# The two-block model on one core: products with v taken as one scheduled step for a pair of heads and a group, changes of form counted in the plan, and whole norms for the scales of w_in

## The chip, the core and the metric

The kernel runs on one core of a Trainium2 chip. The metric is device time in microseconds of one launch, from one execution of the program; several executions are timed and the median is used. The engines are TensorE (PE in the profile, with its weight loads as PEld), VectorE (DVE), ScalarE (ACT), GpSimd (POOL) and SyncE (SP), which here does nothing but issue transfers for the DMA engines.

## The reference, cut to what matters

Attention that is causal in blocks of 64 tokens, a dense layer with an elu between its two products, and a layer of eight experts of which each chosen token visits one:

```python
# q, k, v: (4, 8, 576, 64); x below: (2304, 512)
scores = np.matmul(q, k.transpose(0, 1, 3, 2)) / np.sqrt(D)
scores = np.where(block_i >= block_j, scores, -1e9)
attn = softmax(scores)
x = np.matmul(attn, v)                       # -> (2304, 512)
h = x @ w_in                                 # w_in (512, 2048), float64 in memory
g = np.where(h > 0.0, h, np.exp(np.minimum(h, 0.0)) - 1.0)
x = g @ w_out                                # w_out (2048, 512), float64 in memory
do_compute = x @ w_skip > 0
e_idx = np.argmax(x @ w_gate, axis=1)        # for the tokens with do_compute
out = x + gate_w * (relu(x @ w1[e_idx]) @ w2[e_idx])
```

## The kernel before

**How the work is cut.** The eight heads of a batch element `b` are four pairs `p`. Its nine blocks of 64 tokens are groups `g`: blocks 0 to 3, 4 to 7 and 8 for `b` = 0, and 0 to 3 and 4 to 8 for the others. For every block of a pair TensorE makes scores `s`, VectorE their maximum `mx`, ScalarE the exponential `e`; then the exponentials, scaled, are split into a high and a low fp16 half `ehl`. Two neighbouring blocks share one `ehl`, and a DMA transposes it into `et` (for the first group of `b` = 0 TensorE does that, through `tp`). `y` in the code is such a couple of blocks: 0 and 1 in the first group, 2 to 4 in the second. `pv` multiplies `et` with the split `vt` into the PSUM tile `xps`, which has one buffer (tag `pv`), and ScalarE and VectorE move that into `xt`, the transposed input of the dense layer. The products with v use 64 columns of the array at a time, two heads side by side; so do the scores of block 8. All the rest uses 128 columns. The table `ET_BUFS = 1, 1, 2, 1, 2` gives the number of buffers of `et` for `y` = 0 to 4.

**The dense layer** goes over nine chunks `c` of 256 tokens. `l1` makes `h`, `l1a` and `l1b` the elu `g`, `l2` makes `y`. For the first two chunks the products are in fp32, with `twi` and `two`; from the third on they are three fp16 products of split halves, with `win` and `wout`. The weights come as float64: `raw_load(x)` fetches one of 32 pieces of 512 KB into a raw buffer `rw` (16 pieces of w_in, then 16 of w_out), and `conv(x)` makes fp32 of it with three VectorE instructions. `load_to(n)` issues the loads up to number `n`. The split needs a power of two as a scale for each eighth of w_in. `sq_win(j)` squares the eighth on ScalarE into `sq` (tag `k1`, one buffer, which the splitting of k uses too), adds the squares over the rows of the matrix with four matmuls by ones into `cn` (tag `pv` again), and takes the largest column sum on VectorE. `scale_win` makes the scales of the eight maxima, once. `sq_wout` and `scale_wout` do it in another way for w_out: ScalarE adds up the squares of each partition while it makes them (`accum_out`), and one matmul by ones adds the partitions.

**What sets the order.** Nothing is issued directly. Each instruction is recorded by a `Recorder` as a step, with a time estimate and the tiles that it reads and writes; consecutive TensorE calls are one step until `rc.atom()` ends it. `order()` plays the steps through in a simulated time: at each turn it takes the engine that is free first and of its ready steps the one with the lowest due number, where `rc.base = -300` makes a step due earlier. The steps are then issued in the order of their simulated starts, so each engine's queue is fixed, and the real engines work it off in order, waiting where the plan was wrong. Due numbers come from the program order, which is a list of slots: attention units run ahead of the dense layer by a quota (`SHARE`, `CHUNKS`). TensorE's instructions and all others that pass through the recorder carry the line of its call, L310, in the profile. In `pv` each `y` has an `rc.atom()` ahead of it, so it is a step of its own. `vmax(b)` squares the whole of v of one batch element on ScalarE (`vflat`) for v's scale.

**The end.** After the dense layer the tokens are routed, and the experts follow (`ahead_block`, `block`), from about 606 us on.

Of the kernel before, what the change touches and what calls it, by code (L numbers as in the profile page):

```python
# [34 lines left out]
class Recorder:  # L35
# [15 lines left out]
    def begin(self):  # L51
        self.steps = []
        self.hist = {}
        self.users = {}
        self.rings = {}
        self.masks = {}
        self.cur = None
        self.last_pe = None
        self.shift = self.base = 0
        self.direct = False  # L60
        self.urgent = False
        self.urg = []
        self.late = {}
        self.ready = {}

    def pool(self, p):
        return _Pool(self, p)
# [84 lines left out]
    def order(self):  # L152
# [15 lines left out]
                succ[j].append(i)  # L168
        est = [self.ready.get(i, 0.0) for i in range(n)]
        free = dict(self.late)  # L170
        cand = {}
        dma_free = 0.0
        lanes = []
# [14 lines left out]
        while len(done) < n:  # L188
# [43 lines left out]
            if e == "sp":  # L232
                if len(lanes) >= 8:
                    t = max(t, lanes[-8])
                end = max(t + (1.12 if s[1] < 0.6 else 1.3), dma_free) + s[2]
                dma_free = end
                lanes.append(end + 0.9)
                free[e] = t + s[1]
            else:
                end = t + s[1]  # L240
                if e is not None:
                    free[e] = end
                end += s[2]
# [47 lines left out]
class _Engine:  # L291
# [3 lines left out]
    def __getattr__(self, op):  # L295
        def record(*args, **kw):
            rec, e = self.rec, self.e
            if rec.direct:
                return getattr(self.real, op)(*args, **kw)
            names = {"memset": ("out",), "iota": ("out",), "tensor_copy": ("out", "in_")}.get(op, ())  # L300
            ops = dict(zip(names, args))
            ops.update(kw)
            reads, writes = [], []
            for k, x in ops.items():
                if hasattr(x, "ap") and not hasattr(x, "tensor"):
                    x = x.ap
                if hasattr(x, "tensor"):
                    (writes if k in ("out", "accum_out") else reads).append(x)
            time, dma = self.cost(op, ops)
            rec.call(e, time, lambda: getattr(self.real, op)(*args, **kw), reads, writes, dma)  # L310
        return record

    def cost(self, op, k):
# [34 lines left out]
def tile_kernel(ctx, tc, q, k, v, w_in, w_out, w_skip, w_gate, w1, w2, out):  # L348
# [99 lines left out]
    st = {}  # L448
# [61 lines left out]
    def sq_win(j):  # L510

        if j == 0:
            for nm in ("cwF", "cwS", "cwI", "cwC", "cwM", "cwG"):
                st[nm] = newcol(8).start
        sq = ap.tile([128, 4, 256], BF16, tag="k1", bufs=1, name="sq")
        rc.scalar.activation(out=sq.rearrange("p a b -> p (a b)"), in_=tw("wi", j), func=AF.Square)
        cn = misc([128, 256], "cn", "pv")
        for kk in range(4):
            rc.tensor.matmul(out=cn, lhsT=ones16, rhs=sq[:, kk], start=kk == 0, stop=kk == 3)
        rc.vector.tensor_reduce(out=col[:, st["cwF"] + j:st["cwF"] + j + 1], in_=cn, axis=AX.X, op=ALU.max)  # L520

    def scale_win():

        F_, S_, I_, C_, M_, G_ = (col[:, st[nm]:st[nm] + 8] for nm in ("cwF", "cwS", "cwI", "cwC", "cwM", "cwG"))
        scale_bits(F_, S_, I_)
        rc.vector.tensor_scalar(out=C_, in0=I_, scalar1=st["v", 1][1], scalar2=2.0 ** -14, op0=ALU.mult, op1=ALU.mult)
        rc.vector.tensor_scalar(out=M_, in0=C_, scalar1=2.0 ** 35, scalar2=1.0, op0=ALU.mult, op1=ALU.max)
# [314 lines left out]
    def pv(b, p, g):  # L842
# [3 lines left out]
        for y in range(blk[0] // 2, (blk[-1] + 2) // 2):  # L846
            et = ET.pop((b, p, y))
            n, nk = et.shape[1], et.shape[2] // 2
            c0 = (2 * y - blk[0]) * 64
            rc.atom()  # L850
            for kt in range(nk):
                for eh, vh in ((0, 0), (1, 0), (0, 1)):
                    for h in range(2):
# [462 lines left out]
    rc.base = -300  # L1316
    load_raw("k", 0, 0)
    load_raw("q", 0, 0)
    load_raw("k", 0, 1)
    load_raw("q", 0, 1)  # L1320
    vflat(0)
# [628 lines left out]
```

## Time and profile before

| | us |
|---|---|
| median of 3 runs | 755.23 |
| those runs | 749.65, 756.22, 755.23 |
| profiled execution | 757.81 |
| its span, from the first to the last instruction | 756.1 |
| around the span | 1.7 |
| mean granted clock of TensorE | 0.982 of 2.4 GHz |

The page gives for the whole span each engine's busy time, a strip of 40 slices, and the groups of instructions. Views by stretch, by wait and by time give the rest. Since every instruction has the line of the recorder, groups are told apart by the tiles that they read and write.

### The profile page before, as it was taken

Reading aid. Unit: us, or ns where it says so; the run is one execution under the profiler, and the core shown is the slowest. Engines: PE = TensorE matmul, PEld = TensorE weight load, DVE = VectorE, ACT = ScalarE, POOL = GpSimd, SP = SyncE. Lnnn points to the kernel's source line nnn. Section 1 sums busy time; section 2 is a strip of 40 time slices with the busy share of each in tenths; the row PEclk is TensorE's granted clock in tenths of the full one; section 3 lists DMA queues with packets and bytes.
Section 4 is the critical chain, followed back from the end, with each engine's and each line's share of the span. In section 5 each row is a group of like instructions: output and inputs, shape, how many; then the busy total and the mean of one; then the engine's idle time right before and its main releaser. Section 6 shows DMA issues by size and latency. Waiting matters only on the chain. (4 is left out here: it accounts for less than half of the span.)

```text
span 756.1 us, 17807 instructions
## 1 busy us (share of the span) xinstructions
PE 688.2 (91%) x6696; PEld 471.3 (62%) x6696; DVE 582.8 (77%) x1688; ACT 519.7 (69%) x1100; POOL 84.1 (11%) x122
## 2 busy tenths in 40 slices
PE   4769987899999999988999999999999999997894
PEld 3548633586467666646656666757576677675683
DVE  5987997788899998978859965899778655554662
ACT  5876555799998886877748844767366558584681
POOL 2000000001000100000100010010105033243311
PEclk9999998899999999999999999999999999999998
DMA  9899999887597999879937537927065775989951
GB/s 256 239 236 316 269 251 202 188 150 134 111 192 146 162 190 197 163 131 194 161 53 165 101 63 177 386 67 225 33 196 147 212 169 122 231 195 238 292 145 16
DMA packets 280859, 134.52 MB, mean 178 GB/s; under 512 B 250347, under 2 KB 259061, under 8 KB 280240
## 3 DMA queue, kind: packets, MB, share of 16 engines
q1 hardware_dynamic: 276560, 125.68, 73.4%
q0 software_dynamic: 4192, 7.49, 4.7%
q8 instruction: 57, 0.93, 0.5%
q14 instruction: 50, 0.41, 0.2%
HBM read 74.38 MB, written 12.75 MB: 115 GB/s over the span
## 5 line engine op out<-in xcount | busy, mean ns | idle before, releaser
L310 PE MATMUL h<-xt,win 128*128 128x256 f16 x1344 | 158.4, 273 | 1.5 <-DVE n L310 1.0
L310 PE MATMUL y<-wout,g 128*128 128x512 f16 x672 | 157.0, 381 | 0.0
L310 PEld LDWEIGHTS <-win 128*128 128x128 f16 x1344 | 128.7, 98 | 22.7 <-DVE n L310 1.1
L310 PEld LDWEIGHTS <-g 128*128 128x128 f16 x672 | 64.3, 98 | 67.8 <-issue 2.0
L310 ACT ACTIVATE e<-s,mx 128x512 f32<-128x512 f32 (+4 forms) x160 | 81.9, 514 | 29.7 <-DVE ehl L310 13.5
L310 ACT ACTIVATE ehl<-e,su 128x512 f16<-128x512 f32 (+4 forms) x160 | 80.0, 548 | 15.1 <-DVE su L310 9.5
L310 DVE SCALAR_TENSOR_TENSOR ehl<-e,su,ehl 128x512 f16<-128x512 f32 (+4 forms) x160 | 81.4, 536 | 7.8 <-ACT ehl L310 7.5
L310 DVE TENSOR_REDUCE mx<-s 128x1 f32<-128x512 f32 (+4 forms) x160 | 74.8, 474 | 15.6 <-PE s L310 15.3
L310 PE MATMUL s<-kt,qt 128*128 128x384 f16 (+5 forms) x384 | 71.3, 311 | 11.9 <-ACT e L310 10.1
L310 PE MATMUL h<-xt,twi 128*128 128x256 f32 x256 | 64.0, 406 | 1.4 <-ACT xt L310 1.4
L310 PE MATMUL y<-two,g 128*128 128x512 f32 x128 | 62.6, 626 | 0.5 <-DVE two L310 0.5
L310 PEld LDWEIGHTS <-vt 128*64 128x64 f16 x1440 | 41.4, 115 | 32.4 <-issue 26.6
L310 PE MATMUL xps<-et,vt 128*64 128x128 f16 (+1 forms) x1440 | 50.7, 220 | 11.0 <-DMA et<-ehl 6.4
L310 PEld LDWEIGHTS h<-xt,twi 128*128 128x128 f32 x256 | 50.8, 204 | 9.6 <-ACT xt L310 2.1
L310 PEld LDWEIGHTS <-p 128*128 128x128 f16 x984 | 47.0, 99 | 14.0 <-issue 6.9
L310 ACT ACTIVATE el<-h,col 128x512 f32<-128x512 f32 x56 | 38.2, 682 | 24.7 <-PE h L310 24.3
L310 ACT ACTIVATE g<-el,col 128x512 f16<-128x512 f32 x56 | 40.1, 716 | 13.5 <-DVE el L310 12.8
L310 PEld LDWEIGHTS <-qt 128*128 128x128 f16 (+1 forms) x384 | 28.8, 106 | 28.5 <-issue 13.3
L1509 DVE SCALAR_TENSOR_TENSOR p<-p,n,p 128x1024 f16<-128x1024 f32 x32 | 40.7, 1278 | 4.7 <-ACT p L1508 4.5
L310 DVE SCALAR_TENSOR_TENSOR g<-el,col,g 128x512 f16<-128x512 f32 x56 | 41.6, 742 | 2.4 <-ACT g L310 2.3
L310 DVE SCALAR_TENSOR_TENSOR el<-h,col,el 128x512 f32<-128x512 f32 x56 | 41.6, 744 | 1.6 <-DVE el L310 0.5
L310 POOL DMA_INDIRECT lst_d<-li,si x16 | 18.0, 1126 | 201.5 <-DVE li L310 100.4
(233 smaller groups left out, 1166.3 us busy)
## 6 DMA issues: line engine op xcount, KB each, us to landing
p<-in_moe_w_dram SPq DMA_DIRECT2D x49, 512.0 KB
rw<-in_moe_w_in_dram SPq DMA_DIRECT2D x16, 512.0 KB
rw<-in_moe_w_out_dram SPq DMA_DIRECT2D x16, 512.0 KB
pb<-in_moe_w_dram SPq DMA_DIRECT2D x10, 512.0 KB
vflat<-in_v_dram SPq DMA_DIRECT2D x4, 1152.0 KB
out_dram<-pay SPq DMA_DIRECT2D x18, 256.0 KB
pay_d<-pay SPq DMA_DIRECT2D x18, 256.0 KB
raw<-in_k_dram SPq DMA_DIRECT2D x16, 256.0 KB
```

What stands on the lines that cost most here:

```text
L310: rec.call(e, time, lambda: getattr(self.real, op)(*args, **kw), reads, writes, dma)
L1509: rc.call("dve", 1.2, lambda: nc.vector.scalar_tensor_tensor(out=half(1), in0=raw.t, scalar=sc, in1=half(0), op0=ALU.mult, op1=ALU.subtrac ...
```

## The change

Four things change.

- In `pv` only the first `y` of a group ends the step before it. The products of a pair of heads and a group (18 matmuls in a first group, 42 or 72 in a second) are one step, which is ready when the last of its `et` is there.
- The recorder notes for every matmul whether it is whole (over 64 columns of weights or over 64 output partitions) or half. In the plan a TensorE step costs 0.095 us more when its first matmul has another form than the last one of the step before.
- `sq_win` adds the squares of a partition on ScalarE; `scale_win` adds the partitions of all eight sums with one matmul by ones, between two small VectorE copies. The scale of an eighth comes from the norm of the whole eighth, not of its largest column. The 32 matmuls into `cn` and the eight maxima are gone.
- The first two raw loads of w_in are issued right behind the first k and q.

```diff
+        self.form = {}
@@ order
+        whole = True
...
                 end = t + s[1]
+                if i in self.form:
+                    end += 0.095 * (self.form[i][0] != whole)
+                    whole = self.form[i][-1]
@@ record
-            rec.call(e, time, lambda: getattr(self.real, op)(*args, **kw), reads, writes, dma)
+            i = rec.call(e, time, lambda: getattr(self.real, op)(*args, **kw), reads, writes, dma)
+            if op == "matmul":
+                rec.form.setdefault(i, []).append(_count(ops["lhsT"].ap[1:]) > 64 or ops["out"].ap[0][1] > 64)
@@ sq_win
-        sq = ap.tile([128, 4, 256], BF16, tag="k1", bufs=1, name="sq")
-        rc.scalar.activation(out=sq.rearrange("p a b -> p (a b)"), in_=tw("wi", j), func=AF.Square)
-        cn = misc([128, 256], "cn", "pv")
-        for kk in range(4):
-            rc.tensor.matmul(out=cn, lhsT=ones16, rhs=sq[:, kk], start=kk == 0, stop=kk == 3)
-        rc.vector.tensor_reduce(out=col[:, st["cwF"] + j:st["cwF"] + j + 1], in_=cn, axis=AX.X, op=ALU.max)
+        sq = ap.tile([128, 1024], BF16, tag="k1", bufs=1, name="sq")
+        rc.scalar.activation(out=sq, in_=tw("wi", j), func=AF.Square, accum_out=col[:, st["cwM"] + j:st["cwM"] + j + 1])
@@ scale_win
+        cb = sm.tile([128, 8], BF16, tag="cb8", bufs=1, name="cb")
+        rc.vector.tensor_copy(cb, M_)
+        cn = misc([128, 8], "cn", "pv")
+        rc.tensor.matmul(out=cn, lhsT=ones16, rhs=cb, start=True, stop=True)
+        rc.vector.tensor_copy(F_, cn)
@@ pv
-            rc.atom()
+            if y == blk[0] // 2:
+                rc.atom()
@@ the first loads
     load_raw("k", 0, 0)
     load_raw("q", 0, 0)
+    load_to(2)
     load_raw("k", 0, 1)
```

The plan is played anew, so all engines' queues move up to about 610 us of the run; the experts' part has the same order as before.

On TensorE, the products with v of one pair in the second group of `b` = 1, before (`xps` 64x128 are blocks 4 to 7, 64x64 is block 8, `s` with 64 rows the scores of block 8, `y<-two` the dense layer):

```order
L310 MATMUL xps<-et,vt 64x128
L310 MATMUL y<-two_371,g 128x512 x2
L310 LDWEIGHTS qt
L310 MATMUL s<-kt,qt 64x512
...
L310 LDWEIGHTS vt
L310 MATMUL xps<-et,vt 64x128
...
L310 MATMUL s<-kt,qt 64x64
L310 MATMUL y<-two_371,g 128x512 x2
L310 MATMUL y<-two_389,g 128x512 x2
L310 LDWEIGHTS vt
L310 MATMUL xps<-et,vt 64x64
```

Other work stands between its three parts. Now:

```order
L315 MATMUL s<-kt,qt 64x64
L315 MATMUL y<-two_386,g 128x512 x2
L315 LDWEIGHTS vt
L315 MATMUL xps<-et,vt 64x128
...
L315 MATMUL xps<-et,vt 64x64
L315 LDWEIGHTS qt
L315 MATMUL s<-kt,qt 128x384
```

The three parts now follow each other, behind the scores.

On SP, the loads and transposes ahead of the dense layer's start, about 31 to 43 us of the run, before (`vflat` is v of a whole batch element, `qt` and `kt` the transposed q and k, `raw` their loads):

```order
L310 DMA_TRANSPOSE kt<-k_194 128x8x128
L310 DMA raw<-in_k_dram 64x8x64
L310 DMA_TRANSPOSE qt<-qq 128x16x128
L310 DMA raw<-in_q_dram 64x8x64
L310 DMA raw<-in_v_dram 64x8x64
L310 DMA rw<-in_moe_w_in_dram 128x4x256
L310 DMA vflat<-in_v_dram 128x2304
```

The `vflat` load stands four places behind the transposed q. Now:

```order
L315 DMA_TRANSPOSE kt<-k_194 128x8x128
L315 DMA rw<-in_moe_w_in_dram 128x4x256
L315 DMA raw<-in_k_dram 64x8x64
L315 DMA rw<-in_moe_w_in_dram 128x4x256
L315 DMA wg_79<-in_moe_w_skip_dram 128x4x1
L315 DMA vflat<-in_v_dram 128x2304
L315 DMA_TRANSPOSE qt<-qq 128x16x128
```

Two loads of w_in and that of `vflat` now stand ahead of the transposed q instead of behind it.

On ACT, the last two moves of `xps` into `xt` ahead of the dense layer's start, before:

```order
L310 ACTIVATE xt<-xps,col 128x256
...
L310 ACTIVATE vt<-raw,col 64x8x64
L310 ACTIVATE e_283,su<-s,mx 128x384
L310 ACTIVATE e_286,su<-s,mx 128x384
L310 ACTIVATE vflat,col<-vflat 128x2304
L310 ACTIVATE xt<-xps,col 128x256
```

The last move waits behind the square of `vflat`. Now:

```order
L315 ACTIVATE xt<-xps,col 128x256
L315 ACTIVATE vflat,col<-vflat 128x2304
L315 ACTIVATE qq<-raw 64x8x64 x2
L315 ACTIVATE vt<-raw,col 64x8x64
L315 ACTIVATE k_259<-raw 128x8x64
L315 ACTIVATE e_283,su<-s,mx 128x384
L315 ACTIVATE xt<-xps,col 128x256
```

The square of `vflat`, which stood right ahead of the last move into `xt`, now has five instructions between it and that move.

## Rows read from the trace of the kernel before

**Rows 1.** The page, whole span: busy time, its share, and instructions of each engine.

```profile
PE 688.2 (91%) x6696; PEld 471.3 (62%) x6696; DVE 582.8 (77%) x1688; ACT 519.7 (69%) x1100; POOL 84.1 (11%) x122
```

**Rows 2.** By stretch: length, busy time of PE, PEld, DVE, ACT, POOL, granted clock, DMA share, GB/s.

```profile
0.00:48.00 48.00, 27.54 (x238) 18.94 (x240) 37.07 (x111) 35.34 (x82) 4.14 (x39) 1.00 0.96 248
48.00:104.00 56.00, 54.02 (x260) 37.41 (x255) 47.81 (x99) 31.94 (x58) 0.00 (x0) 1.00 1.03 273
104.00:132.00 28.00, 21.17 (x127) 9.61 (x128) 23.31 (x56) 16.05 (x32) 0.20 (x1) 0.88 1.06 218
160.00:465.00 305.00, 293.01 (x2892) 192.10 (x2891) 256.93 (x814) 233.27 (x567) 15.68 (x24) 0.99 0.81 144
```

**Rows 3.** By stretch, around an idle time of the transfers.

```profile
35.40:38.50 3.10, 1.68 (x14) 1.13 (x14) 3.10 (x10) 3.10 (x6) 0.00 (x0) 1.00 0.00 0
38.50:121.40 82.90, 74.83 (x385) 47.97 (x385) 73.67 (x156) 48.71 (x97) 0.35 (x1) 0.98 1.08 268
```

**Rows 4.** Tile `cn`: instructions, duration in ns (least, median, most), first and last start.

```profile
L310 PE MATMUL cn<-sq,ones x32: 269/272/282, 74.9 to 136.1; 128*128 128x256 bf16 x32
L310 DVE TENSOR_REDUCE col<-cn x8: 402/419/425, 80.1 to 136.4; 128x1 f32<-128x256 f32 x8
```

**Rows 5.** Timeline (start, length, engine) around one set of `cn`.

```profile
117.37 0.60 PE L310 MATMUL cn<-sq,ones 128*128 128x256 bf16 x4
117.90 0.68 PE L310 MATMUL s<-kt,qt 128*64 128x512 f16 x8
```

**Rows 6.** Timeline around the last piece of w_out.

```profile
125.06 0.43 DVE L310 TENSOR_SCALAR two<-rw 128x512 int32<-128x512 int32 x1 [1.70 <-DMA rw<-in_moe_w_out_dram]
126.74 0.68 DVE L310 SCALAR_TENSOR_TENSOR two<-rw,two 128x512 int32<-128x512 int32 x1
127.31 0.60 PE L310 MATMUL cn<-sq,ones 128*128 128x256 bf16 x4 [3.59 <-ACT sq L310]
127.75 0.97 PE L310 MATMUL y<-two,g 128*128 128x512 f32 x1
```

**Rows 7.** Timeline of PE across changes of form; then the page's group of `y`.

```profile
399.67 1.47 PE L310 MATMUL y<-wout,g 128*128 128x512 f16 x6
401.07 0.68 PE L310 MATMUL s<-kt,qt 128*64 128x512 f16 x8
...
L310 PE MATMUL y<-wout,g 128*128 128x512 f16 x672 | 157.0, 381 | 0.0
```

**Rows 8.** Timeline of SP's issues ahead of the dense layer's start.

```profile
32.86 0.74 SPq L310 DMA_DIRECT2D raw<-in_k_dram  x1
37.32 1.33 SPq L310 DMA_TRANSPOSE qt<-qq  x1
...
41.48 0.45 SPq L310 DMA_DIRECT2D vflat<-in_v_dram  x1
```

**Rows 9.** Timeline of PE and ACT at the dense layer's start.

```profile
50.12 2.12 ACT L310 ACTIVATE vflat<-vflat 128x2304 f32<-128x2304 f32 x1 [3.49 <-DMA vflat<-in_v_dram]
52.75 0.79 PE L310 MATMUL h<-xt,twi 128*128 128x256 f32 x1 [1.35 <-ACT xt L310]
```

**Rows 10.** PE's waits, 160 to 465 us: total, times, longest.

```profile
PE xps L310 <- DMA et<-ehl: 6.4, 5, 2.0
```

**Rows 11.** By stretch: two of the five with a granted clock of 0.50.

```profile
110.80:114.20 3.40, 3.40 (x16) 1.21 (x16) 3.00 (x7) 2.75 (x6) 0.00 (x0) 0.50 1.03 268
141.50:148.30 6.80, 5.97 (x50) 4.77 (x50) 5.35 (x23) 5.87 (x20) 0.20 (x1) 0.50 0.71 186
```

**Rows 12.** Timeline: SP's issues of `et`, and a product that waits for one.

```profile
161.95 1.33 SPq L310 DMA_TRANSPOSE et<-ehl  x1
166.05 1.22 SPq L310 DMA_TRANSPOSE et<-ehl  x1
...
322.45 1.32 SPq L310 DMA_TRANSPOSE et<-ehl  x1
329.13 1.44 PE L310 MATMUL xps<-et,vt 128*64 128x128 f16 x24 [2.05 <-DMA et<-ehl]
```

## Prediction

> **What bounds the kernel now.** The page comes first. TensorE is busy 688.2 of 756.1 us [rows 1], so the time is TensorE's work plus what it idles; the question is where a shorter queue of its own would only wait longer. The view by stretch answers that [rows 2]. From 160 to 465 us TensorE is busy 293.0 of 305 us: there every 0.1 us taken from its queue should come off the end. From 0 to 48 us it is busy 27.5 of 48, from 104 to 132 us 21.2 of 28, while the DMA share is about 1. The transfers are what is late there: between 1.9 and 121 us they stand still once for long, 3.1 us at 35.4 [rows 3], and VectorE waits 1.70 us for the last piece of w_out, converts it until 126.74 + 0.68 = 127.42 us, and the product that needs it starts at 127.75 [rows 6]. What is saved on TensorE before 125 us is therefore mostly not saved; what moves that load is.
>
> The profiled execution took 757.8 us (756.1 and 1.7 around the span), which is 2.6 more than the median of 755.2. I make the sum against the profiled one and take it off the median.
>
> **The whole norms.** Gone are 32 matmuls and eight maxima [rows 4]. One set of four matmuls holds TensorE from 117.37 until the next work starts at 117.90, 0.53 us, and in that is one change of form (0.09, below), so a set costs 0.44 us and eight cost 3.5 us [rows 5]. Five sets (74.9 to 117.4 us) lie before the last piece of w_out and hide behind it, as above; three lie behind it: 1.3 us. Added is one small matmul, at most the 0.27 us of a wide one [rows 4]: 1.0 us stay. The wait of 3.59 us ahead of one set [rows 6] looks like the bigger gain. It isn't: the product behind it needs the piece whose conversion ends at 127.42, and the set starts at 127.31. Without the set TensorE waits for VectorE instead, and the gain is the 0.33 us between 127.42 and 127.75 at best. VectorE loses eight maxima of 0.42 us, 3.4 us, and gains two copies of a column; from 104 to 132 us it is busy 23.3 of 28, so I count 0.5 us of it. ScalarE must read eight accumulators out; it is busy 31.9 of 56 us and 16.1 of 28 there [rows 2], which covers it, and it no longer waits for TensorE to give the squares' buffer back. If that cover were gone, a read of one column is hardly dearer than a maximum over 256, 0.42 us [rows 4], so 3.4 us at most. I take 1.5 us for this part, between 0.5 and 7 (all eight sets and the wait).
>
> **The joined steps and the counted changes.** Six products of 512 columns start at 399.67 and end at 401.14; one alone is 0.38 long, so the last starts at 400.76 and five steps took 1.09, 0.218 each. The next matmul could start at 400.98 and starts at 401.07, in the other form [rows 7]: 0.09 us lost at the change, and the diff's own figure is 0.095. Counted along TensorE's order up to the experts, there were 160 changes and now there are 122. Of the 38 that go, eight lie ahead of the dense layer's first product, where TensorE idles anyway, eight in the first two chunks, 22 behind. I count half of the middle ones and all of the last: (4 + 22) x 0.095 = 2.5 us, between 2.1 and 3.6.
>
> The Trainium skill, page "TensorE: Matmul & The Clock Gate", section "Step-by-step: what each phase is for", says that TensorE pulls weight loads ahead of matmuls in flight, so that the next weights load beside the running product. By that rule alone a change of form would cost nothing and this term would be 0. The row shows 0.09 us, so it doesn't hold across a change; the page "TensorEngine Tiling (Array Packing)", section "Key Properties", says that changing the mode drains the engine, and with that the trace agrees.
>
> A joined step waits for the last of its transposes, where each part waited for its own. Now 6.4 us go into five such waits [rows 10]. There were 80 places where one could come, now there are 36, and the early parts of a step get slack. In proportion 3.5 us would go; but the wait for the last part is as long as before, and all the step's work stands behind it. I take 1.5 us, between 3 lost and 3.5 gained.
>
> **The first loads.** Two loads of 512 KB move ahead of the second k, of v of batch element 0 and of the second q. At 248 to 273 GB/s [rows 2] they take about 4 us together, and the second k and `vflat` come that much later. The products of the first units with v need v's scale, but stand later in TensorE's order than before, so I count nothing. VectorE gets two conversions to do early, when it idles. What I count is at 32 to 52 us. SP sits from 33.6 to 37.3 us on a transposed q whose input isn't ready, and the transfers run dry [rows 3, 8]. Behind it stands `vflat`, issued at 41.48; ScalarE waits 3.49 us for it, squares it in 2.12, and only then moves `xt`, for which the dense layer's first product waits until 52.75 [rows 8, 9]. Now two loads of w_in and `vflat` stand ahead of that q, and five instructions stand between the square and the move. So up to 3.5 us of ScalarE's wait go, and TensorE starts the dense layer that much earlier; and up to 3.1 us of dry transfers are filled. Of the first only what the transfers also give passes 127 us. Against it, two more raw loads and one transposed k now stand ahead of the last piece of w_out: 0.26 MB each at 273 GB/s, about 1 us each, though that is work that is then done. I take 1.7 us, half of 3.5, between 0 and 3.8.
>
> **The clock.** In five stretches the granted clock is 0.50, the lower of its two levels, 1.2 GHz: four of about 3.4 us and one of 6.8 at 141.5 [rows 11]. One of 3.4 us costs half of itself, 1.7 us. Three lie between 104 and 160 us, where TensorE idles most (the clock of 104 to 132 us is 0.88 [rows 2]) and should idle less. I take half of one, 0.9 us, between 0 and 6.8 (half of 3.4 + 3.4 + 6.8).
>
> **The sum.** 1.5 + 2.5 + 1.5 + 1.7 + 0.9 = 8.1 us: 757.8 becomes 749.7, and the median of 755.2 becomes **747.1**.
>
> **The rivals.** *The transfers hide it.* If the load of w_out's last piece doesn't move, the norms, the first loads and the clock give only the 1.0 us behind it, and the joined steps 2.5: 755.2 - 3.5 = 751.7. For it speaks the DMA share of 1.03 to 1.08 up to 121 us [rows 2, 3]; against it the 3.1 us of dry transfers.
>
> *Everything passes.* The dense layer starts 3.5 us earlier and the stage keeps it, all eight sets count with 3.5, two slow stretches go (3.4), the changes give 3.6: 14 us, 741. Against it speaks the same DMA share.
>
> *Held buffers, slower.* `et` of the first couple of blocks has one buffer. It was free when its own product was done; now it is free when the whole pair's is. The next pair's transpose into it stands on SP, and raw loads and all further transposes queue behind it. The gap from the second `et` of one pair to the first of the next is 4.1 us at 161.95. A transpose was waited for until 6.7 us after its issue (322.45 to 329.13), and the product behind it took 1.4 [rows 12]: 8.1 - 4.1 = 4.0 us that SP would stand still, at nine such places (three in each of three first groups), 36 us. It decides once the exponentials' buffers are full, so that ScalarE stops; if half of it arrives at TensorE, 18 us, and with 5 us of the gains left the time is 755.2 + 18 - 5 = 768. Against it: the plan knows this dependence and sets the transposes later, and at its latest the gap in the second group is much longer.
>
> *The change doesn't do what it says.* The order shows that it does; what can fail is only that the new order has new waits of its own, which is in the ranges.
>
> *Changes of form are free.* If the weights of the next form loaded beside the last product of the old, the 0.09 us would be no loss of the change and the 2.5 us would not come: 749.6. The gap [rows 7] stands against it.
>
> This is the rule of the Trainium skill cited above, page "TensorE: Matmul & The Clock Gate".
>
> **How the numbers follow.** About 1%, 7.5 us, is what a measurement of this kernel can tell from no change; the three runs alone lie 6.6 us apart. The forecast has 0.42, hidden transfers 0.28, everything passes 0.15, held buffers 0.10, free changes 0.05. Faster by over 1% is below 747.7: the forecast lies on that edge, a little more than half of it falls below (0.24), and nearly all of the third (0.15), with 0.06 from hidden transfers and new luck of the order: 0.45. Slower by over 1% is nearly all of the held buffers, 0.09. The rest, 0.46, is the same. The range takes in hidden transfers with 5 us of new waits and nearly all of "everything passes": 740 to 757; outside lie the held buffers and the tails, under 0.2.
>
> **What the profile after would show.** Some 36 products with v that start in one piece, and TensorE's idle time in front of them on `et` under 6.4 us; else the fourth term is wrong. The dense layer's first long run at about 49 us instead of 52.75, and no wait of ScalarE for `vflat` there; else the third. The conversion of the last piece of w_out at 122 to 125 us instead of 125.06; if it is at 125 or later, hidden transfers is right. The stretch from the first chunk with fp16 weights to the experts shorter by 3 to 4 us. Fewer than five stretches at 0.50. The prediction is wrong above all if SP waits long for TensorE in the first groups, or if a new order of loads leaves VectorE without w_out.

## The result, and the profile of the changed kernel

The changed kernel takes 758.71 us in the median of 14 runs (754.82 to 764.81), the kernel before 753.40 in 14 runs beside it. The ratio is 1.0075 (95% interval 1.0048 to 1.0101): slower by three quarters of a percent, where 747.1 us was forecast and 740 to 757 was the range. Ratios here leave out the runs that took over 1.5% longer than the fastest one of their kernel. The profiled execution took 755.88 us, 754.1 of them the span. It is one of the faster draws of its kernel, as the 757.81 before is one of the slower ones there. So the two totals are not compared, and of two places the time from one to the next counts for more than the lead at either.

Most of what the prediction named did happen. The page's busy times [rows 1] and the view by stretch [rows 2], with the stretch between the attention and the experts added:

```profile
PE 676.6 (90%) x6665; PEld 464.3 (62%) x6665; DVE 582.3 (77%) x1682; ACT 519.1 (69%) x1108; POOL 81.0 (11%) x122
```

```profile
48.00:104.00 56.00, 50.30 (x236) 32.94 (x236) 50.41 (x105) 36.10 (x73) 0.00 (x0) 1.00 1.11 272
104.00:132.00 28.00, 21.47 (x169) 9.88 (x169) 23.96 (x78) 16.21 (x37) 0.20 (x1) 1.00 1.07 243
160.00:465.00 305.00, 293.46 (x2948) 194.67 (x2947) 259.31 (x813) 229.33 (x558) 15.82 (x24) 1.00 0.79 146
465.00:606.00 141.00, 135.21 (x1049) 90.33 (x1048) 114.11 (x345) 86.24 (x131) 17.59 (x24) 0.99 0.54 171
```

From 160 to 465 us TensorE is busy as before. From 465 to 606 us it is busy 135.2 of 141 us, where the kernel before has 140.0. At the dense layer's start the timeline shows `vflat` squared at 42.22 without a wait and the products `h` behind the last `xt` at 48.75 instead of 52.75 [rows 9]; the last piece of w_out is converted at 123.28 instead of 126.74 [rows 6]:

```profile
42.22 2.12 ACT L315 ACTIVATE vflat<-vflat 128x2304 f32<-128x2304 f32 x1
48.75 0.70 PE L315 MATMUL h<-xt,twi 128*128 128x256 f32 x2 [1.50 <-ACT xt L315]
123.28 0.68 DVE L315 SCALAR_TENSOR_TENSOR two<-rw,two 128x512 int32<-128x512 int32 x1
```

PE's waits from 160 to 465 us [rows 10]: half of the waits for `et` are gone, and the scores wait longer for the exponentials (2.1 us before):

```profile
PE s L315 <- ACT e L315: 4.9, 9, 0.8
PE xps L315 <- DMA et<-ehl: 3.2, 3, 2.1
```

Where the lead goes is seen in a table of starts on TensorE, read from the timelines of four kernels. The last two belong to experiments below: the changed kernel with a third buffer for one small tile, `li`, and the kernel before with the whole norms and the early loads alone.

| start on TensorE, us | before | changed | changed, third `li` | norms and loads |
|---|---|---|---|---|
| chunk 1's last product | 218.19 | 210.74 | 210.39 | 211.32 |
| last product with v | 464.19 | 455.66 | 455.02 | 450.69 |
| chunk 6's last product | 507.93 | 503.75 | 497.43 | 494.43 |
| chunk 8's last product | 592.64 | 587.85 | 581.15 | 579.14 |
| first product of the experts' loop | 618.29 | 614.46 | 607.13 | 604.76 |
| end of the profiled execution | 757.81 | 755.88 | 744.31 | 747.08 |

The changed kernel leads by 8.5 us at its last product with v and by 4.2 us one chunk later. How much of the 8.5 is a gain can't be told from these two profiles: the counted changes alone, which measure like the kernel before (0.9990, below), lead it by 4.3 us at the same place, and by 4.2 at the end. The loss doesn't hang on that: from the last product with v to chunk 6's last product it takes 48.09 us, where the kernel before takes 43.74. What stands between is a stall of three engines, here in the timeline of GpSimd, VectorE, ScalarE and TensorE (engine by engine; in brackets the idle time ahead and what ended it; the rows of one engine follow each other with others between):

```profile
471.26 1.22 POOL L315 DMA_INDIRECT lst_d<-li,si  x1 [38.05 <-DVE li L315]
477.90 0.97 POOL L315 DMA_INDIRECT lst_d<-li,si  x1 [5.42 <-DMA lst_d<-li,si]
...
483.27 0.17 DVE L315 COPY li<-tokid 128x2 f32<-128x2 f32 x1 [4.53 <-DMA lst_d<-li,si]
485.50 0.15 DVE L315 CAST cb<-n 128x1 bf16<-128x1 f32 x1
...
484.16 0.72 ACT L315 ACTIVATE g<-el,col 128x512 f16<-128x512 f32 x1 [3.55 <-DVE el L315]
...
481.35 1.46 PE L315 MATMUL y<-wout,g 128*128 128x512 f16 x6
485.71 0.16 PE L315 MATMUL ns<-cb,ones 128*128 128x1 bf16 x1 [2.90 <-DVE cb L315]
```

`route2` writes the list rows of a chunk (token number and gate) into `li`, and two indirect transfers on GpSimd scatter them into `lst_d`. `li` has two buffers, so chunk 7 gets chunk 5's. At 471.26 chunk 5's first scatter is issued; the second has to wait for it and goes at 477.90, 5.42 us after the first was out of GpSimd's hands. VectorE has chunk 7's copy of the token numbers next in its queue and stands for 4.53 us until the second scatter has left the buffer. ScalarE then waits for `el`, and TensorE for `cb`, the norm of a piece of expert weights, 2.90 us, behind which its `y` is queued. The view by stretch shows why the scatter is slow, and what the clock did next:

```profile
465.00:471.00 6.00, 6.00 (x49) 4.24 (x48) 5.39 (x34) 5.42 (x11) 0.00 (x0) 1.00 1.02 402
471.00:477.00 6.00, 6.00 (x42) 3.84 (x41) 5.97 (x12) 2.77 (x5) 1.22 (x1) 1.00 1.05 398
477.00:483.00 6.00, 5.81 (x39) 3.72 (x38) 1.72 (x5) 3.32 (x5) 0.97 (x1) 1.00 1.04 392
485.00:488.40 3.40, 2.69 (x8) 1.03 (x8) 3.40 (x6) 3.40 (x5) 0.00 (x0) 0.50 0.02 7
```

Through both scatters the transfers run at a share above 1 and some 400 GB/s: the first expert weights, 512 KB a piece. After the wait the granted clock is 0.50, 1.2 GHz, for 3.4 us.

In the kernel before the same two scatters of chunk 5 are there, and come when the weights are in. GpSimd's timeline, and the stretch that begins 0.7 us after the first was issued:

```profile
491.30 1.22 POOL L310 DMA_INDIRECT lst_d<-li,si  x1 [49.82 <-DVE li L310]
494.38 0.97 POOL L310 DMA_INDIRECT lst_d<-li,si  x1 [1.86 <-DMA lst_d<-li,si]
...
492.00:498.00 6.00, 6.00 (x42) 3.85 (x40) 6.00 (x7) 6.00 (x8) 1.48 (x2) 1.00 0.07 20
```

The second scatter waits 1.86 us there instead of 5.42, and VectorE copies at 498.03 with no wait.

### The profile page after: what moved, and what is told of

Its sections match the earlier page's. It is cut to its first block, busy times and chain, and to the rows that moved or that the text cites. A ratio compares the mean times of both kernels' runs of the same rounds, so it can differ in the third digit from the quotient of the medians.

```text
span 754.1 us, 17731 instructions
## 1 busy us (share of the span) xinstructions
PE 676.6 (90%) x6665; PEld 464.3 (62%) x6665; DVE 582.3 (77%) x1682; ACT 519.1 (69%) x1108; POOL 81.0 (11%) x122
## 5 line engine op out<-in xcount | busy, mean ns | idle before, releaser
L315 ACT ACTIVATE e<-s,mx 128x512 f32<-128x512 f32 (+4 forms) x160 | 82.0, 515 | 23.4 <-DVE ehl L315 11.6
L315 PE MATMUL s<-kt,qt 128*128 128x384 f16 (+5 forms) x384 | 70.7, 308 | 20.0 <-ACT e L315 16.9
L315 PE MATMUL y<-two,g 128*128 128x512 f32 x128 | 60.1, 603 | 5.0 <-DVE two L315 5.0
L315 PE MATMUL h<-xt,twi 128*128 128x256 f32 x256 | 61.0, 390 | 2.3 <-ACT xt L315 1.5
L315 PEld LDWEIGHTS h<-xt,twi 128*128 128x128 f32 x256 | 48.2, 194 | 10.3 <-DVE g L315 2.2
L315 PEld LDWEIGHTS <-vt 128*64 128x64 f16 x1440 | 38.8, 114 | 20.6 <-issue 18.0
L315 PE MATMUL xps<-et,vt 128*64 128x128 f16 (+1 forms) x1440 | 44.7, 217 | 7.3 <-DMA et<-ehl 5.9
L315 PEld LDWEIGHTS y<-two,g 128*128 128x128 f32 x128 | 22.9, 189 | 30.5 <-issue 18.0
```

Source lines behind the costliest of these rows:

```text
L315: i = rec.call(e, time, lambda: getattr(self.real, op)(*args, **kw), reads, writes, dma)
```

## The experiments

Ratios are to the kernel before on the same chip, with 95% intervals; absolute times of different groups are not compared, since they ran on different chips. Three theories stood at the start: *late loss* (the early gain is real and given back behind the attention), *joined steps cost* by themselves, and *luck of the order* (any new plan meets other waits).

### Each part alone

n_only puts the new `sq_win` and `scale_win` into the kernel before, j_only the condition ahead of `rc.atom()` in `pv`, f_only the lines with `form`, l_only the line `load_to(2)`; each diff is that part of the diff above.

> The kernel before with the whole norms alone; loads, steps of the products with v and the plan's costs as before. Three theories for the whole change's 0.75% loss. Late loss: the early gain is real and is given back after 453 us, where the re-dealt order holds TensorE on the scales of the expert weights; then this part, which takes 3.5 us of TensorE's work away before 140 us, shows chunk 1's last product 1 to 4 us earlier, and a time of 0.995 to 1.000 of before. Joined steps cost: the loss is theirs alone, so this is 0.995 to 1.000 too, with no give-back after 453 us. Luck of the order: what a new plan meets is worth up to 1% either way, whatever was edited; then this lies anywhere from 0.993 to 1.010, and its last products of chunk 1 do not tell where it ends.

> The kernel before with the joined steps alone (120 changes of form instead of 160 up to the experts, 36 runs of products with v instead of 68). Joined steps cost: 1.006 to 1.012 of before, and TensorE's waits of scores for the exponentials go from 10 to some 17 us, as in the changed kernel. Late loss: 0.996 to 1.002 by 453 us, and what is lost is lost behind that. Changes of form are worth their 0.095 us each: 3 us earlier at chunk 8's last product. Luck of the order: anywhere from 0.993 to 1.010.

> The kernel before with the counted changes of form alone (152 changes instead of 160). By the price of a change this is worth under 1 us, 0.999 to 1.000. Luck of the order: the plan is another one from the first products on, and the time moves by more than the 1 us that the change pays, up to 1% either way; that is the theory that this run tells from the other two, which both expect no difference here.

> The kernel before with the two early raw loads alone (172 changes of form instead of 160). By the prediction's term the dense layer's first long run starts 3 to 4 us earlier and 1.7 us of it stays: 0.995 to 1.000. Late loss: the early lead is there at 450 us and half of it or more is gone at the end. Luck of the order: the dense layer starts earlier and the end does not follow, anywhere from 0.993 to 1.010.

Measured: norms 0.9963 (0.9935 to 0.9991), joined 1.0018 (0.9989 to 1.0046), counted 0.9990 (0.9962 to 1.0017), loads 0.9952 (0.9919 to 0.9985). The sum of the four is -0.8%; together they are +0.75%. So no part is bad by itself in the size that is to be explained, and two of them gain what late loss expected. Joined steps alone show the stall as well (VectorE 4.16 us at `li`, TensorE 2.7 us at `ns`), and no gain to speak of from 40 changes of form fewer. The kernels without joined steps have neither wait.

### The parts in company

n_l has norms and loads; the next two leave one part out of the changed kernel; the last is the changed kernel with another price:

```diff
-                    end += 0.095 * (self.form[i][0] != whole)
+                    end += 0.1 * (self.form[i][0] != whole)
```

> Whole norms and early loads, without the joined steps and without counted changes of form. The two alone measured 0.9963 and 0.9952 of before. If the parts add up, 0.990 to 0.994, and the loss then belongs to the joined steps and the counted changes in company with these. If the luck of the order decides, no sum holds: 0.993 to 1.008. Late loss: chunk 1's last product 7 to 12 us earlier than before, and less at the end.

> The changed kernel with the products of a couple of blocks as steps of their own again. Joined steps cost: the loss goes, 0.988 to 0.996 of before. Late loss by the re-dealt order, whoever re-dealt it: 1.000 to 1.008, and the scale of expert weights holds TensorE again near 480 us. Luck: anywhere from 0.990 to 1.008.

> The changed kernel without the counted changes of form. By the price of a change this costs under 1 us: the joined steps keep the count low. Joined steps cost: 1.003 to 1.010 of before as the changed kernel. Luck: another order with the same work, anywhere from 0.990 to 1.008.

> The changed kernel, where a change of form counts 0.100 us in the plan instead of 0.095. No work differs; a fifth of TensorE's instructions stand elsewhere in the queue. Joined steps cost, and late loss by what the edits do: as the changed kernel, 1.004 to 1.010 of before. Luck of the order: it differs from the changed kernel by 0.4% or more, either way; this run tells the luck from the other two.

Measured: norms and loads 0.9886 (0.9849 to 0.9922), all but joined 0.9954 (0.9922 to 0.9986), all but counted 1.0004 (0.9971 to 1.0037), price 0.100 1.0035 (1.0004 to 1.0066). Norms and loads add up (0.9963 x 0.9952 = 0.9915, inside the interval). Joining costs 1.2% beside them, with the counting (0.9954 to 1.0075) or without (0.9886 to 1.0004); counting at 0.095 costs 0.7%, with joining or without. The other price moves the time by 0.4% with no work changed, about the error of such a difference; what the luck of the order can be worth is seen from the pace kernels below. The wait at `li` is 4.16 to 4.63 us in the four profiles with joined steps and absent in the six without, the kernel before among them; that is a coincidence of plans until it is taken away by itself.

### The wait taken away

Three kernels get a third buffer, so that chunk 7 doesn't need chunk 5's. Up to the stall their order is that of their pairs:

```diff
-        li = sm.tile([128, 2, 2], F32, tag="li", bufs=2, name="li")
+        li = sm.tile([128, 2, 2], F32, tag="li", bufs=3, name="li")
```

The fourth run of the group is about the counting: all but joined, with the price at 0.100.

> The changed kernel with three buffers instead of two for li, the list rows that two scatters carry out for each routed chunk. TensorE's order stays but for some 220 lines near the stall. In the traces so far the four kernels with joined steps have VectorE waiting 4.2 to 4.6 us at 480 to 488 us for a scatter to leave its buffer, and TensorE 2.7 to 3.0 us behind it; the four without have neither. Late stall: both waits go, the stretch from the last product with v to chunk 6's last product shrinks from 48 to some 43.7 us, and the time is 0.4 to 0.6% below the changed kernel, 1.002 to 1.004 of before. If the stall is only covered by another (the loads of expert weights or the payload's loads come no earlier), 1.006 to 1.009 as the changed kernel.

> Whole norms, early loads and joined steps, without counted changes, and three buffers for li. The same without the third buffer measured 1.0004 of before. Late stall: 0.993 to 0.997; it then explains about half of the 1.2% that joining costs against the kernel with norms and loads alone (0.9886). If the stall is covered by another wait: 0.999 to 1.002.

> Whole norms and early loads with three buffers for li, as a control: here the scatter is out before VectorE needs its buffer, and no wait stands there in the trace. Late stall: no difference from 0.9886, 0.986 to 0.991. If the third buffer helps in some other way than by the stall, this gets faster as well. If 0.9886 was a lucky order, this one, which differs little in it, says nothing; but the time should repeat within 0.3%.

> Whole norms, early loads and counted changes, where one counts 0.100 us instead of 0.095; some 7% of TensorE's lines move. Counted without the joined steps measured 0.9954, 0.7% above norms and loads alone, although its plan has 154 changes of form instead of 162. If the counting itself makes the plan worse (it trades a saved change for a later start of something waited for), this is 0.994 to 0.997 again. If the 0.7% is the luck of one order, this lies elsewhere, 0.986 to 0.993.

Measured: changed with a third `li` 0.9955 (0.9920 to 0.9991) against 1.0075 without; all but counted with it 0.9895 (0.9852 to 0.9938) against 1.0004; the control, norms and loads, 0.9898 (0.9857 to 0.9940) against 0.9886, the same. The stall costs 1.1 to 1.2%, twice what was expected, and in the control, which has no stall, the buffer is worth nothing. The counting at the other price 0.9986 (0.9955 to 1.0016): with 0.9954 at the first, both above the 0.9886 without. So the loss isn't that of one unlucky order; whether it comes of what is counted or of any other timing in the plan, this doesn't tell. From the last product with v to chunk 6's last product, the view by stretch of the changed kernel and of the one with the third buffer:

```profile
455.66:503.75 48.09, 45.19 (x345) 30.45 (x338) 39.08 (x94) 29.42 (x45) 2.19 (x2) 0.96 0.55 198
```

```profile
455.02:497.43 42.41, 42.41 (x334) 28.96 (x327) 37.74 (x91) 28.53 (x44) 2.25 (x2) 1.00 0.63 224
```

48.09 becomes 42.41, with TensorE busy throughout: 5.7 us. 2.9 are the wait, 1.3 the half clock of 2.69 busy us behind it. The other 1.3 are work that moved: up to 500.07 TensorE's order is the same in both; there the changed kernel has 12 products `h` of a later chunk ahead of chunk 6's last product, the other behind it, so that the next stretch, to chunk 7's last product, is shorter in the changed kernel (39.82 us against 41.27).

```profile
500.07 1.47 PE L315 MATMUL h<-xt,win 128*128 128x256 f16 x12
503.75:543.57 39.82, 39.82 (x296) 26.59 (x295) 35.34 (x96) 21.75 (x30) 2.25 (x2) 1.00 0.46 139
```

```profile
497.43:538.70 41.27, 41.27 (x308) 27.67 (x307) 37.03 (x99) 23.35 (x32) 1.93 (x2) 1.00 0.44 129
```

So the place itself costs 4.3 us. All but counted, which has the wait (3.00 us) and no fall of the clock, bears that out: 47.10 us against 42.40 with the third buffer, and the same 12 products moved. The scatter is as slow as before, only nobody waits for it; GpSimd with the third buffer:

```profile
470.69 1.28 POOL L315 DMA_INDIRECT lst_d<-li,si  x1 [38.14 <-DVE li L315]
477.38 0.97 POOL L315 DMA_INDIRECT lst_d<-li,si  x1 [5.41 <-DMA lst_d<-li,si]
```

More is lost later. From chunk 7's last product to chunk 8's, with the same products in both, the changed kernel takes 1.8 us longer. It waits 1.5 us for `x2t`, the transposed rows that the routing of a chunk reads, and with the third buffer not at all; in the second pair of profiles (below) it is 1.5 us longer, with 1.1 us of that wait against none. The first pair, the changed kernel's stretch and wait, then the other's stretch:

```profile
543.57:587.85 44.28, 42.81 (x321) 28.77 (x320) 32.75 (x90) 25.95 (x36) 10.69 (x16) 1.00 0.58 175
PE lp L315 <- DMA x2t<-pay: 1.5, 2, 1.0
```

```profile
538.70:581.15 42.45, 42.45 (x320) 28.93 (x319) 32.00 (x90) 25.29 (x35) 10.85 (x16) 1.00 0.65 204
```

With 0.6 us more up to the first product of the experts' loop that makes 6.7 us since the last product with v (158.80 against 152.11), and the two kernels are 7.3 us apart. There ScalarE has to wait until an output scatter of the experts has left its buffer, and TensorE's first matmul on `mxwo` comes behind that; the changed kernel, then the one with the third buffer:

```profile
622.99 0.47 ACT L315 ACTIVATE o<-y,gp 128x256 f32<-128x256 f32 x1 [4.69 <-DMA out_dram<-o,ah]
623.57 5.82 PE L315 MATMUL hp<-mxwo,p 128*128 128x128 f16 x72 [3.39 <-ACTq L1800]
625.00:628.40 3.40, 3.40 (x36) 3.40 (x34) 0.42 (x1) 1.51 (x4) 0.30 (x1) 0.50 0.73 228
```

```profile
614.29 0.47 ACT L315 ACTIVATE o<-y,gp 128x256 f32<-128x256 f32 x1 [3.31 <-DMA out_dram<-o,ah]
614.86 4.19 PE L315 MATMUL hp<-mxwo,p 128*128 128x128 f16 x72 [2.01 <-ACTq L1800]
```

1.4 us more of wait, and here a second fall of the clock, 1.7 us. In the second pair of profiles (below) TensorE's wait is 3.06 against 1.67 us, without that fall. Why the output scatter is later there wasn't tried.

### The wait taken away in another way, and the pace of the plan

all_li_pool leaves the two buffers and lets GpSimd make the copy that VectorE waited in; j_only_li3 is the kernel before with joined steps and a third buffer. The pace kernels are all_but_counted_li3 with a flat price in the plan, for every step of TensorE, which has nothing to do with form:

```diff
-        rc.vector.tensor_copy(li[:, :, 0], tokid[:, 2 * c:2 * c + 2])
+        rc.gpsimd.tensor_copy(out=li[:, :, 0], in_=tokid[:, 2 * c:2 * c + 2])
```

```diff
-                    end += 0.095 * (self.form[i][0] != whole)
-                    whole = self.form[i][-1]
+                    end += 0.0208
```

> The changed kernel, where the token numbers are copied into li by GpSimd instead of VectorE; li keeps its two buffers. GpSimd issued the scatters itself and has nothing else to do then; VectorE's second copy into li (the gate) comes much later. Late stall: VectorE's wait of 4.5 us and TensorE's of 2.9 us go as with the third buffer, and the time falls from 1.0075 to 0.994 to 0.998 of before. If the third buffer gained by another order of the rest, this stays at 1.003 to 1.009.

> The kernel before with the joined steps and three buffers for li. Joined steps alone measured 1.0018. If the stall is the whole price of joining and as dear here as there, 0.990 to 0.994, and joining is then worth 0.6 to 1% by itself, of which the 40 changes of form fewer at 0.09 us make 0.5%. If joining is worth nothing without the stall, as all_but_counted_li3 against n_l_li3 says, 0.998 to 1.000, and the stall cost little here.

> Norms, loads, joined steps and three buffers for li; instead of 0.095 us for a change of form, the plan adds 0.0208 us to every step of TensorE, the same 11 us in all. Without any of it: 0.9895. With the price of form: 0.9955. If the price costs by making TensorE slower in the plan, so that the plan's steps meet inputs that are late on the chip, 0.993 to 0.998. If it costs by where the changes of form are, 0.988 to 0.991.

> The same with 0.0208 us taken off every step of TensorE in the plan. If the pace of the plan is what costs, the other sign gives 0.985 to 0.989, or stays within 0.2% of 0.9895 if nothing waits there any more. If any other plan than the tuned one is worse, as the luck of the order has it, 0.992 to 1.000.

Measured: copy on GpSimd 0.9934 (0.9910 to 0.9957), joined with a third `li` 0.9955 (0.9926 to 0.9983), pace added 0.9993 (0.9953 to 1.0034), pace taken off 1.0008 (0.9979 to 1.0038). The first of the four settles the wait. GpSimd's timeline shows who waits now:

```profile
479.67 0.97 POOL L315 DMA_INDIRECT lst_d<-li,si  x1 [5.40 <-DMA lst_d<-li,si]
485.03 1.04 POOL L315 COPY li<-tokid 128x2 f32<-128x2 f32 x1 [4.39 <-DMA lst_d<-li,si]
```

The wait for the buffer is there, 4.39 us; it stands on an engine that nobody waits for, and the time falls by 1.4%. Joined steps alone gain 0.6% by the third buffer, less than the 1.1 to 1.4% in company, and then stand 0.45% under the kernel before, which neither of the two expected ranges held. Of the pace, my theory fell: added or taken off, it costs 1.0 to 1.1% against the 0.9895 of the kernel without it, so it isn't the direction. The plan's time estimates give a good order as they are, and 11 us more or less, spread over the plan, give a worse one. No work differs in these kernels, so the luck of the order is worth 1% here, about as much as the stall and no less than the 0.3 to 1.0% that counting costs in the company of other parts. That counting costs by what it counts is therefore not shown. The price of the stall rests on more than such ratios: the traces show it place by place, 4.3 us before the orders of the two kernels part.

Where counting loses was read from two profiles, PE's waits from chunk 2's first to chunk 3's last product, without counting (212.73 to 332.96, 120.2 us) and with it (213.04 to 336.02, 123.0 us), both with the third `li`:

```profile
PE lp L310 <- DMA x2t<-pay: 1.0, 2, 0.8
PE s L310 <- ACT e L310: 0.2, 1, 0.2
```

```profile
PE s L315 <- ACT e L315: 3.0, 5, 1.0
PE lp L315 <- DMA x2t<-pay: 2.1, 2, 1.3
```

The scores wait 2.8 us longer for the exponentials, all other waits together 1.0 us less. That isn't the loss in general: without joined steps the same stretch takes 120.57 us in norms and loads and 125.52 with counting at 0.100, and the scores wait 0.6 and 0.8 us there. This was read and not tried.

### The changed kernel and the third buffer side by side

> The changed kernel once more: 1.004 to 1.010 of before, VectorE's wait of 4 to 5 us for a scatter's buffer near 480 us again, and 48 us from the last product with v to chunk 6's last product.

> The changed kernel with three buffers for li once more, on the same chip: 0.993 to 0.998 of before, 0.9 to 1.3% below the changed kernel, no wait at li, and 42 to 44 us from the last product with v to chunk 6's last product.

Measured: the changed kernel 1.0087 (1.0056 to 1.0119), with the third `li` 0.9942 (0.9904 to 0.9979), 760.16 and 750.72 us in the median of 12 runs each on one chip: 9.4 us. The wait is there again, 4.43 us at 483.95 in the first and none in the second. The two profiles are 0.8 us apart the other way at the last product with v, 5.7 us at the experts' loop and 6.9 at the end; the pair before ends 11.6 us apart.

The fastest kernels are norms and loads alone (0.9886, and 0.9898 with the third buffer), and norms, loads and joined steps with the third buffer (0.9895). Between them there is no difference to be measured. Put in one after the other, norms and loads take off 1.1% (0.9886), joined steps with their stall add 1.2% (1.0004), and counting adds 0.7% (1.0075).

## Why the prediction was wrong

**The step that failed** is the one on new waits: "what can fail is only that the new order has new waits of its own, which is in the ranges". One such wait costs 8 to 11 us with what follows from it, as much as or more than all the gains of the sum (8.1), and it stands behind 465 us, where the prediction priced nothing. It used 160 to 465 us as the stretch where every 0.1 us comes off the end, and took it for granted that what is gained there stays. In the changed kernel's own trace it doesn't. Three experiments beside norms and loads that take VectorE out of that wait give 1.1 to 1.4% back, and the pair run side by side 1.4%; with joined steps alone it is 0.6%.

**A second step failed to the other side**: "What is saved on TensorE before 125 us is therefore mostly not saved". Norms and loads were to give 1.5 + 1.7 = 3.2 us together, with most of their work hidden behind the load of w_out's last piece. They give 1.1%, 8.6 us, and not by that piece: they convert it at 125.91, and with the third buffer, as fast, at 127.42, where the kernel before has 126.74.

**How it comes about.** The buffers of the attention are given back together, when their last users are done, and then SP issues 16 pieces of expert weights. In norms and loads alone three of them go at 452.11, ahead of chunk 5's payload on SP, and the others from 458.47; in the changed kernel all go from 461.54, behind the payload:

```profile
452.11 1.46 SPq L1460 DMA_DIRECT2D p<-in_moe_w_dram  x3
...
458.47 0.46 SPq L1460 DMA_DIRECT2D p<-in_moe_w_dram  x1
```

```profile
461.54 1.96 SPq L1468 DMA_DIRECT2D p<-in_moe_w_dram  x4
```

Chunk 5's first scatter goes at 477.80 in the one and at 471.26 in the other. The weights come 3 to 9 us later, the routing 6.5 us earlier, and the scatter falls into the stream of weights; in norms and loads alone it comes at the end of the stream, and the second goes 1.92 us after the first:

```profile
472.00:478.00 6.00, 6.00 (x46) 4.13 (x44) 6.00 (x29) 5.38 (x7) 0.20 (x1) 1.00 1.04 387
478.00:484.00 6.00, 6.00 (x41) 3.87 (x40) 6.00 (x8) 6.00 (x9) 1.99 (x2) 1.00 0.06 21
```

The plan counts 2 us for a scatter whatever else is under way. Why joining brings the routing forward and the weights back wasn't looked for. The Trainium skill, page "DMA: Bandwidth & Descriptors", section "Queues, rings and completion order", says that each DMA engine takes turns between its queues, a whole packet at a time. By that rule a small scatter waits for packets of the weights on the engines that it shares with them. The trace agrees in that the scatter is slower in the stream, 5.42 us against 1.86 without it in the kernel before; that the turns make the difference isn't shown.

**Held buffers** was the rival of the right kind at the wrong place: a buffer that is free only when a transfer is out, and a queue that stands still for it. It was looked for on SP at `et`. SP's waits for `xps` from 45 to 465 us are 16.9 us before and 16.7 after.

**The terms, one by one.** *Whole norms*, 1.5 us forecast: alone 0.37% of 755, 2.8 us, inside the bounds of 0.5 to 7. *First loads*, 1.7 us: alone 0.48%, 3.6 us (1.1 to 6.1 by the interval); the steps were right as far as the profile of the changed kernel shows them (the start 4.0 us earlier, no wait for `vflat`, the last conversion 3.5 us earlier), but the last conversion is not what passes the gain on, as said above. *The clock*, 0.9 us: neither shown nor refuted. Between 104 and 160 us, where it was expected, the changed kernel has one stretch at 0.50, of 6.9 us (133.4 to 140.3), instead of three of 13.6 together; its second profile has two, of 10.2 together, so one profile doesn't tell. Behind 465 us it has three of 3.4 us (485.0, 625.0 and 693.2) instead of one, and the first is the one at the stall. A fifth, from 24.2 to 44.7 us, has no counterpart, since the profile before lacks the clock of its start (last section). *Fewer waits for `et`*, 1.5 us: they fell by 3.2 us as in proportion, and the waits for the exponentials rose by 2.8. *Changes of form*, 2.5 us: not there. Joining alone removes them (160 to 120) and its worth without the stall is 0 beside norms and loads (0.9895 against 0.9898) and 0.45% alone. Counting alone leaves 152 of the 160, and beside the other parts it costs 0.3 to 1.0%. The prediction priced the two as one, as if the plan avoided what it counts. It doesn't: counted along TensorE's order in the traces, up to the experts' loop, all but counted has 116 changes and the changed kernel 124. `order()` takes the ready step with the lowest due number, and the price enters only the time at which TensorE is free again. That could be read in the code.

*Hidden transfers* (751.7) is refuted by the norms and loads, which gain 1.0 to 1.1% whether the last conversion moves or not; its sum also left out the 1.5 us of fewer waits without a reason, with which it would be 750.2. *Free changes of form* is refuted as to the price of one: in the trace of the kernel before, from 145 to 600 us, a matmul of the same form starts 0.216 us after a `y` of 512 columns (median of 35 places, `h` or `s` next) and one of the other form 0.309 us after it (21 places, `xps` or `s` next), 0.093 us more. What 40 fewer are worth to the whole stays open: they would be 3.7 us, 0.5%, and without the stall the joined steps gave 0.45% alone and nothing in company.

**What is not settled:** the stall costs 9.4 us in the medians of the pair run side by side. In the first pair of profiles 4.3 us are at its place, 2.4 follow up to the experts' loop, and 3 are named behind that; whether the waits for `x2t` and for the output scatter come of the stall, or of the order that differs in the two kernels from 500 us on, was not tried. Nor is it settled whether counting loses by what it counts, and by which wait.

## What to carry to other kernels

When a planner re-deals an order, ask of each small tile that a transfer empties who waits for its buffer, and with what else in flight; one more buffer of a few bytes decided 1.2% here. A gain that is kept for 450 us says nothing of the end, so look at the transitions between phases, where many buffers come free at once. A new order with the same work was worth 1% here, so a theory on a wait is tested by taking away that wait and leaving the rest of the order. And a cost in a plan is worth having only if the choice of the next step can react to it.

## What the runs showed of the hardware

The second scatter of the pair could go 1.4 to 1.9 us after GpSimd had issued the first (128 rows of 8 bytes) when the transfers were nearly idle, and 4.8 to 5.4 us after it beside 512 KB loads at 400 GB/s; each of the 20 profiles shows the one or the other at this place (8 without joined steps, 12 with them), by whether the weights were in. And the clock in a row can be wrong at a profile's start: the row of the kernel before for 0 to 48 us gives 1.00 [rows 2], while in its timeline six `h` of 128x256 took 2.93 us at 48.47; in the changed kernel, whose rows give 0.50 from 24.2 to 44.7 us, the same six took 1.56 us at 45.69, right after the clock rose. In the second profile with the third buffer the rows give 0.50 from 32.8 to 53.3 us, and there the six took 2.93 us at 46.05. So the mean granted clock of 0.982 for the kernel before is too high, and its stretches at 0.50 are more than the five counted.
